# Shift-times-V summed on VectorE, the text shift made by matmul rows, the text gate moved into the output phase

## The chip, the core and the metric

The kernel runs on one core of one Trainium2 chip. The metric is the device time of one execution in microseconds (us). A profiled execution spans about 1.8 us less than that time, because the span runs from the first instruction to the last (117.0 against 118.8 us for the profiled run of before). "Before" and "after" (the changed kernel) are the two kernels compared.

## The reference

The work is an attention block with two token streams, image (256 tokens) and text (32), for B = 2 batches, with D = 1152 and all data in bf16:

```
mod_i, mod_t = silu(c) @ wmod_img, silu(c) @ wmod_txt       # shift, scale, gate of each stream
hi = layernorm(x_img) * (1 + sci) + shi ;  ht = layernorm(x_txt) * (1 + sct) + sht
qkv_i = hi @ wqkv_img ;  qkv_t = ht @ wqkv_txt
q, k, v = concat(text, image)                               # 288 tokens
a = softmax(q @ k.T * D**-0.5) @ v
out_i = x_img + gai * (ai @ wo_img) ;  out_t = x_txt + gat * (at @ wo_txt)
```

Twelve weight blocks of 1152 x 1152 are modulation or projection blocks and two are output blocks. Each is 2.65 MB, and together they are 37 of the 41 MB that a run moves.

## The kernel before

Each weight block goes into one of five slots. A load into a slot must wait until the last reader of its earlier content is done, so the table of slots is also a table of waits (in the profile they are waits of SyncE, which issues the loads: the longest in after was 12.8 us, for matmuls that read the slot):

```python
w_sc_i = wtile(0); w_v_i = wtile(1)
w_sh_i = load_w(2, wmod_img, 0)
w_q_i = load_w(3, wqkv_img, 0)
w_sh_t = load_rows(0, wmod_txt, 0)
w_k_i = load_w(4, wqkv_img, D)
w_sc_t = load_w(1, wmod_txt, D)          # waits for w_v_i
w_q_t = load_w(2, wqkv_txt, 0)           # waits for w_sh_i
w_k_t = load_w(3, wqkv_txt, D)           # waits for w_q_i
w_ga_i = load_w(0, wmod_img, 2 * D)      # waits for w_sh_t
w_v_t = load_w(1, wqkv_txt, 2 * D)
w_ga_t = load_w(2, wmod_txt, 2 * D)
w_o_i = load_rows(3, wo_img, 0)
w_o_t = load_rows(1, wo_txt, 0)
```

The image V is made without its shift, to start early. The missing term s = shi @ Wv is the same for each token of a batch, and softmax rows sum to 1, so s can be added as a bias to the attention output. The text tokens have no such term, so s is subtracted from the text V. Before gets s on TensorE, and gets the *text* shift as a sum on VectorE (DVE), folded by 16 small matmuls:

```python
def mod_rows_of(w, lhs):                          # 36 matmuls, four column groups side by side
    gps = ps_tr.tile([P, KT, LW], f32, tag="tr")
    for kt in range(KT):
        for g in range(NGG):
            mm(gps[LW*g:LW*g+LW], lhsT=lhs[:, kt, :], rhs=group(w, kt, g), ...)
    return gps
def shift_v_rows():
    p_sv = mod_rows_of(w_v_i, shT32)              # shift @ Wv on TensorE
    nc.scalar.copy(svr[:], p_sv[:])
    cols["v"] = mod_cols_of(p_sv, "svc")
def vec_part(eng, w, acc, r0, r1, bs): ...        # text shift: 18 multiply-adds on DVE over w_sh_t
def v_txt(r):
    ...                                           # 18 matmuls for the text V, then
    for g in range(2):                            # two that subtract s inside PSUM
        mm(ps[64*g:64*g+NTT], lhsT=sel[:, 2*r+g, :], rhs=svr[:], start=False, stop=True, ...)
...
vt = [v_txt(r) for r in range(2)]
v_txt_out(0, vt[0]); p_transposes(0); p_transposes(1); v_txt_out(1, vt[1])
txt_gate()                                        # 36 matmuls, then gate rows through DRAM
for d0 in range(0, KT, 3): attn_pair(...)
out_img(0, C3); out_img(1, C3); out_img(2, C3); out_txt(); out_img(3, ...)
```

## Time and profile before

| what | number | where it is read |
|---|---|---|
| time | 118.58 us, median of 5 | timing runs |
| TensorE (PE) busy | 111.2 of 117.0 us | first part of the page |
| weight queue busy | 87% of the span | DMA queues on the page |
| PE stages near the attention | below | timeline of PE |

These lines are from the page of before: the busy time of each engine, then rows of the span cut into 40 slices of 2.9 us. PE and DMA are tenths of the slice, where 9 is 90% or more; GB/s is what the DMA engines moved.

```profile
PE 111.2 (95%) x1046; PEld 63.9 (55%) x1054; DVE 74.6 (64%) x158; ACT 44.4 (38%) x91; POOL 11.1 (10%) x34
PE   4998899999999999999999999999999999999990
DMA  3999999999999999999999999999999999520223
GB/s 98 368 374 390 409 407 409 411 410 414 411 399 372 410 410 413 404 411 413 413 410 413 414 402 414 414 401 414 408 406 411 406 401 376 177 100 6 101 50 101
```

PE is full from the sixth slice on. The weight stream is full too: about 400 to 414 GB/s, with one dip to 372, until slice 33.

The next lines are from the timeline of PE in before. The columns are start in us, length in us, then engine, line, operation, tile written, tiles read and count.

```profile
64.25 1.29 PE L61 MATMUL gps<-t,sT 128*32 128x288 bf16 x36
65.36 0.66 PE L61 MATMUL gps<-hl,pick 128*32 128x288 bf16 x16
66.18 3.83 PE L61 MATMUL ps<-xT_i,t 128*128 128x512 bf16 x17 [0.16 <-issue]
...
86.64 1.29 PE L61 MATMUL gps<-t,sT 128*32 128x288 bf16 x36
87.85 0.91 PE L61 MATMUL aps<-pT,v_i 128*128 128x288 bf16 x6
88.69 0.42 PE L61 MATMUL aps<-pT,v_t 32*128 32x288 bf16 x6
89.04 1.65 PE L61 MATMUL aps<-pT,v_i 128*128 128x288 bf16 x12
```

The 36 matmuls at 86.64 are the text gate. The attention (tiles aps) follows at 87.85; its small matmuls on v_t, the text V, take 0.35 us from start to next start. Nothing waits.

These lines are from the DMA view of before: issuing queue, size of each transfer, and median us from issue to landing.

```profile
gbf<-mod_scratch POOLq DMA_DIRECT2D x4, 36.0 KB, 4.8
mod_scratch<-g_sb POOLq DMA_DIRECT2D x4, 2.2 KB, 6.1
```

### The profile page before, as it was taken

What the parts mean: (1) busy time and instruction counts of PE and PEld (TensorE: products, weight loads), DVE (VectorE), ACT (ScalarE), POOL (GpSimd) and SP (SyncE); (2) the same over time, 40 slices, a digit from 0 to 9 for tenths busy, and PEclk for the clock granted to TensorE, in tenths of its full rate; (3) what the DMA queues carried; (4) which work ended last, traced back from release to release, by engine and by line L of the source; (5) the groups of instructions that cost most, each with busy time, mean ns of one, the idle gap of its engine ahead of it and who ended that gap; (6) DMA issues with size and microseconds to landing.
All of it is one profiled execution on the core that took longest, in us unless ns stands there. A gap on an engine that the chain in (4) does not pass through costs nothing.

```text
span 117.0 us, 2513 instructions
## 1 busy us (share of the span) xinstructions
PE 111.2 (95%) x1046; PEld 63.9 (55%) x1054; DVE 74.6 (64%) x158; ACT 44.4 (38%) x91; POOL 11.1 (10%) x34
## 2 busy tenths in 40 slices
PE   4998899999999999999999999999999999999990
PEld 1245544445574444445444658777876666656660
DVE  2368694053867979999996350018984756666671
ACT  4599720042654834325265224245556610000000
POOL 7230000000000000000000000001318018000000
PEclk9999999999999999999999999999999999999998
DMA  3999999999999999999999999999999999520223
GB/s 98 368 374 390 409 407 409 411 410 414 411 399 372 410 410 413 404 411 413 413 410 413 414 402 414 414 401 414 408 406 411 406 401 376 177 100 6 101 50 101
DMA packets 18613, 40.86 MB, mean 349 GB/s; under 512 B 1019, under 2 KB 1547, under 8 KB 18603
## 3 DMA queue, kind: packets, MB, share of 16 engines
q1 hardware_dynamic: 17728, 39.56, 87.0%
q0 software_dynamic: 480, 0.89, 2.1%
q10 hardware_dynamic: 395, 0.26, 0.7%
q8 instruction: 8, 0.13, 0.4%
q14 instruction: 2, 0.02, 0.0%
HBM read 39.38 MB, written 1.34 MB: 348 GB/s over the span
## 4 chain that ended last, share of the span: by engine, by line
PE 85%; ACT 5%; DMA 4%; DVE 2%; issue 1%; DVEq 0%
PE ps L61 53%; PE vps L61 15%; PE gps L61 6%; PE aps L61 5%; PE sps L61 4%; DMA x_i<-in_x_img_dram 4%; ACT xn_i L202 2%; ACT xn_i L201 2%; PE pT_ps L64 1%; DVE xn_i L216 1%; PE tp L64 1%; DVE tmp L690 1%; ACT rstd L211 1%; ACT rstd L212 1%; DVE o L691 0%
## 5 line engine op out<-in xcount | busy, mean ns | idle before, releaser
L61 PE MATMUL ps<-xT_i,t 128*128 128x512 bf16 x157 | 35.2, 380 | 0.4 <-issue 0.2
L61 PEld LDWEIGHTS <-t 128*128 128x128 bf16 x324 | 20.5, 98 | 19.1 <-issue 0.5
L427 DVE SCALAR_TENSOR_TENSOR acc_sh<-t,sTf,acc_sh 128x1152 f32<-128x1152 bf16 x16 | 21.4, 1414 | 0.0
L61 PE MATMUL ps<-t,aT 128*128 128x384 bf16 (+3 forms) x153 | 20.2, 308 | 0.0
L61 PE MATMUL vps<-t,hS_i 128*128 128x512 bf16 (+1 forms) x106 | 17.8, 325 | 0.2
L61 PEld LDWEIGHTS <-aT 128*128 128x128 bf16 (+1 forms) x153 | 13.0, 101 | 7.1 <-issue 0.5
L61 PEld LDWEIGHTS <-hS_i 128*128 128x128 bf16 x108 | 9.0, 98 | 8.8 <-DVE hS_i L268 0.5
L690 DVE TENSOR_TENSOR tmp<-ps,gb 128x384 bf16<-128x384 f32 (+2 forms) x13 | 6.8, 526 | 6.3 <-PE ps L61 6.3
L370 ACT CAST qkT<-ps 128x512 bf16<-128x512 f32 (+2 forms) x11 | 6.0, 552 | 11.0 <-PE ps L61 11.0
L61 PE MATMUL wps<-warm 128*128 128x512 bf16 x24 | 8.1, 498 | 1.7 <-DVE unit L132 1.5
L515 POOL DMA_DIRECT2D mod_scratch<-g_sb x4 | 2.5, 633 | 74.6 <-ACT g_sb L513 74.5
L368 ACT ACTIVATE qkT<-ps 128x512 bf16<-128x512 f32 (+2 forms) x11 | 6.1, 559 | 9.1 <-PE ps L61 9.1
L184 DVE CAST v_i<-vps 128x512 bf16<-128x512 f32 x5 | 3.5, 692 | 7.5 <-PE vps L61 7.5
L554 DVE TENSOR_REDUCE nmx<-sps 128x1 f32<-128x288 f32 x4 | 1.8, 458 | 9.9 <-PE sps L61 9.9
L186 ACT CAST v_i<-vps 128x512 bf16<-128x512 f32 x4 | 2.3, 578 | 10.0 <-PE vps L61 10.0
L623 DVE TENSOR_SCALAR aT<-aps,svc 128x288 bf16<-128x288 f32 x9 | 4.3, 518 | 2.5 <-PE aps L61 2.5
L61 PEld LDWEIGHTS <-warm 128*128 128x128 bf16 x25 | 2.7, 118 | 5.5 <-issue 2.9
L61 PEld LDWEIGHTS <-sT 128*32 128x32 bf16 x180 | 4.6, 96 | 2.0 <-issue 1.3
L61 PE MATMUL sps<-qkT 128*128 128x288 bf16 (+1 forms) x54 | 5.5, 287 | 0.0
L61 PE MATMUL gps<-t,sT 128*32 128x288 bf16 x144 | 5.2, 287 | 0.0
L61 PE MATMUL aps<-pT,v_i 128*128 128x288 bf16 x36 | 5.1, 288 | 0.0
L61 PE MATMUL ps<-hT_t,t 128*128 128x64 bf16 x162 | 5.1, 193 | 0.0
(114 smaller groups left out, 109.2 us busy)
## 6 DMA issues: line engine op xcount, KB each, us to landing
t<-in_wqkv_txt_dram SPq DMA_DIRECT2D x3, 2592.0 KB, 17.8
t<-in_wmod_img_dram SPq DMA_DIRECT2D x2, 2592.0 KB, 13.0
t<-in_wqkv_img_dram SPq DMA_DIRECT2D x2, 2592.0 KB, 20.1
t<-in_wmod_txt_dram SPq DMA_DIRECT2D x2, 2592.0 KB, 15.9
t<-in_wmod_txt_dram SPq DMA_DIRECT2D x3, 864.0 KB, 14.7
t<-in_wo_img_dram SPq DMA_DIRECT2D x3, 864.0 KB, 12.8
t<-in_wo_txt_dram SPq DMA_DIRECT2D x3, 864.0 KB, 12.6
t<-in_wqkv_img_dram SPq DMA_DIRECT2D x3, 576.0 KB, 9.1
```

Source lines behind the costliest of these rows:

```text
L61: return pin(nc.tensor.matmul(*a, **k))
L64: return pin(nc.tensor.transpose(*a, **k))
L184: nc.vector.tensor_copy(out_ap, in_ap)
L186: nc.scalar.copy(out_ap, in_ap)
L201: pin(nc.scalar.activation(junk, x_ap, ACT.Copy, scale=1.0 / D, accum_out=sm[:, 0:1]))
L202: pin(nc.scalar.activation(junk, x_ap, ACT.Square, scale=float(D) ** -0.5, accum_out=sm[:, 1:2]))
L368: nc.scalar.mul(out_ap, in_ap, SCALE)
L370: nc.scalar.copy(out_ap, in_ap)
L427: pin(eng.scalar_tensor_tensor(acc[:, b, :], w[:, kt, :], sTf[:, kt, b:b + 1], acc[:, b, :], op0=ALU.mult, op1=ALU.add))
L515: nc.gpsimd.dma_start(gsc[si, b, :].rearrange("(g j) -> g j", g=NGG), g_sb[b:P:32, :])
L623: nc.vector.tensor_scalar(dst, tiles[(b, dt)][:], bias, None, op0=ALU.add)
L690: nc.vector.tensor_mul(tmp[:, 0:n], ps[:, 0:n], gb[:, b, c0:c0 + n])
```

## The change

The intent: TensorE is the bound (95% busy), and DVE has idle time (64% busy), so shift-times-V (36 matmuls) moves to DVE. The author held that DVE has no time for two such sums, so the text shift goes back to TensorE. Cut to its core:

```diff
-    w_sc_t = load_w(1, wmod_txt, D)
-    w_q_t = load_w(2, wqkv_txt, 0)
-    w_k_t = load_w(3, wqkv_txt, D)
-    w_ga_i = load_w(0, wmod_img, 2 * D)
+    w_sc_t = load_w(2, wmod_txt, D)
+    w_q_t = load_w(3, wqkv_txt, 0)
+    w_k_t = load_w(0, wqkv_txt, D)
+    w_ga_i = load_w(2, wmod_img, 2 * D)
     w_v_t = load_w(1, wqkv_txt, 2 * D)
-    w_ga_t = load_w(2, wmod_txt, 2 * D)
-    w_o_i = load_rows(3, wo_img, 0)
-    w_o_t = load_rows(1, wo_txt, 0)
+    w_o_i = load_rows(4, wo_img, 0)
+    w_ga_t = load_w(3, wmod_txt, 2 * D)
+    w_o_t = load_rows(0, wo_txt, 0)
 ... (w_q_i now in three pieces, w_sh_t in one)
-    def shift_v_rows(): ...                       # and the DVE sum of the text shift
+    def sv_part(r0, r1): ...                      # 18 DVE multiply-adds over w_v_i into acc_sv
+    def sv_blocks(): ...                          # per batch a 32x32 block transpose and a reduce_sum
+    def sv_fold(): ...                            # two matmuls with `fold`; gives svc, the bias
+    def sv_rows():
+        ps = ps_tr.tile([B * KT, P], bf, tag="tr", name="svr")
+        tr(ps[:], svcb[:].rearrange("p b k -> p (b k)"), ident[:])
+        pin(nc.scalar.copy(srow[:], ps[:]))
+        nc.gpsimd.dma_start(svd[:, :].rearrange("b (k p) -> (b k) p", p=P), srow[:])
+        for g in range(2):
+            for b in range(B):
+                r0 = 64 * g + NT * b
+                nc.gpsimd.dma_start(svb[r0:r0 + NT, :], svd[b, g * HD:(g + 1) * HD].partition_broadcast(NT))
     def txt_rows_shift():
-        ...                                       # 16 fold matmuls
+        rows["sh"] = mod_rows_of(w_sh_t, sT32)
     def v_txt_out(r, ps):
-        ...                                       # copies; the two sel matmuls of v_txt go too
+        pin(nc.vector.tensor_sub(v_t[:, r * VC:(r + 1) * VC], ps[:], svb[:, r * VC:(r + 1) * VC]))
+        if r == 0:
+            pin(nc.vector.tensor_sub(v_t[0:NTT, HD:HD + NTT], ps[NTT:P, 0:NTT], svb[NTT:P, 0:NTT]))
 ...
-    qk_img(w_q_i, 0, {1: (txt_stats, txt_shift_part(0, 3),), 3: (txt_norm,), 4: (txt_shift_part(3, 6),),
-                      7: (txt_shift_part(6, KT),)})
-    qk_img(w_k_i, 1, {1: (txt_transposes, txt_shift_split,),
-                      6: (txt_rows_scale, txt_rows_shift, txt_cols_shift, txt_modulate),
-                      8: (lambda: qk_txt(0, w_q_t),)})
+    qk_img(w_q_i, 0, {0: (txt_stats, sv_part(0, 3)), 3: (txt_norm,), 4: (sv_part(3, 6),), 8: (sv_part(6, KT),)})
+    qk_img(w_k_i, 1, {1: (txt_transposes,),
+                      3: (txt_rows_scale, txt_rows_shift, txt_cols_shift, txt_modulate, sv_blocks),
+                      8: (lambda: qk_txt(0, w_q_t), sv_fold)})
+    sv_rows()
     qk_txt(1, w_k_t)
 ...
-    v_txt_out(0, vt[0]); p_transposes(0); p_transposes(1); v_txt_out(1, vt[1]); ...
-    txt_gate()
+    p_transposes(0)
+    for r in range(2):
+        v_txt_out(r, v_txt(r))
+    p_transposes(1)
     attention
     out_img(0, C3)
+    txt_gate()
     out_img(1, C3)
```

The sum s now reaches the text V through DRAM (store, then four broadcast loads into svb). And w_v_i stays in its slot until DVE is done with it, so the later blocks had to change slots.

More of the change, by code (lines that the diff above doesn't have):

```diff
@@ L111 @@
     w_sh_i = load_w(2, wmod_img, 0)
-    w_q_i = load_w(3, wqkv_img, 0)
-    w_sh_t = load_rows(0, wmod_txt, 0)
+    w_q_i = load_rows(3, wqkv_img, 0)
+    w_sh_t = load_w(0, wmod_txt, 0)
     w_k_i = load_w(4, wqkv_img, D)
-    w_sc_t = load_w(1, wmod_txt, D)
-    w_q_t = load_w(2, wqkv_txt, 0)
-    w_k_t = load_w(3, wqkv_txt, D)
-    w_ga_i = load_w(0, wmod_img, 2 * D)
+    w_sc_t = load_w(2, wmod_txt, D)
+    w_q_t = load_w(3, wqkv_txt, 0)
+    w_k_t = load_w(0, wqkv_txt, D)
+    w_ga_i = load_w(2, wmod_img, 2 * D)
     w_v_t = load_w(1, wqkv_txt, 2 * D)
-    w_ga_t = load_w(2, wmod_txt, 2 * D)
-    w_o_i = load_rows(3, wo_img, 0)
-    w_o_t = load_rows(1, wo_txt, 0)
+    w_o_i = load_rows(4, wo_img, 0)
+    w_ga_t = load_w(3, wmod_txt, 2 * D)
+    w_o_t = load_rows(0, wo_txt, 0)
     nc.scalar.preload_act_table_set("natural_log_exp_and_others")
@@ L144 @@
     sTf = const.tile([P, KT, B], f32)
-    pick = const.tile([P, B, 32], bf)
-    nc.gpsimd.memset(pick[:], 0.0)
-    for b in range(B):
-        nc.gpsimd.memset(pick[:, b, b:b + 1], 1.0)
-    shT32 = const.tile([P, KT, 32], bf)
-    nc.gpsimd.memset(shT32[:], 0.0)
     PBW = 3 * P
@@ L162 @@
     nc.gpsimd.tensor_copy(ident2[:, P - NT:P], ident[:, 0:NT])
+    fold = const.tile([P, NGG, LW], bf)
+    nc.gpsimd.tensor_add(fold[:, 0, :], ident[:, 0:LW], ident[:, LW:2 * LW])
+    for g in range(2, NGG):
+        nc.gpsimd.tensor_add(fold[:, 0, :], fold[:, 0, :], ident[:, g * LW:(g + 1) * LW])
+    for g in range(1, NGG):
+        nc.gpsimd.tensor_copy(fold[:, g, :], fold[:, 0, :])
     e18 = small.tile([B * KT, P], f32, bufs=1)
@@ L227, in mod_cols_of @@
     def mod_cols_of(gps, name):
-        t = const.tile([P, KT, LW], f32, name=name, tag={"shtc": "scc", "sctc": "shc"}.get(name, name))
+        t = const.tile([P, KT, LW], f32, name=name, tag={"shtc": "scc"}.get(name, name))
         pin(nc.vector.transpose(t[:].rearrange("p c l -> p (c l)"), gps[:].rearrange("p c l -> p (c l)")))
@@ L344 @@
     sh_i = mod_cols_of(p_sh, "shc")
-    nc.vector.tensor_copy(shT32[:, :, 0:B], sh_i[:, :, 0:B])
     hT_i = xT_i
@@ L382 @@
     gsc = tc.dram_tile([2, B, D], bf, name="mod_scratch")
-    sel = const.tile([P, NGG, NTT], bf)
-    nc.gpsimd.tensor_scalar(sel[:].rearrange("p g (b t) -> p g b t", b=B),
-                            ident[:].rearrange("p (g r) -> p g r", g=NGG)[:, :, 0:B].unsqueeze(3)
-                            .to_broadcast([P, NGG, B, NT]), -1.0, None, op0=ALU.mult)
-    v_t = act.tile([P, D], bf)
-    svr = act.tile([P, KT, LW], bf)
+    svd = tc.dram_tile([B, D], bf, name="sv_scratch")
+    HD = D // 2
+    v_t = act.tile([P, HD + NTT], bf)
+    svb = act.tile([P, HD], bf)
     rows, cols = {}, {}
-    def shift_v_rows():
-        p_sv = mod_rows_of(w_v_i, shT32)
-        nc.scalar.copy(svr[:], p_sv[:])
-        cols["v"] = mod_cols_of(p_sv, "svc")
     xT_t = act.tile([P, KT, NTT], bf)
@@ L402, in txt_stats @@
     def txt_stats():
-        junk = v_t[0:NTT, :]
+        junk = work.tile([P, D], bf, tag="o", name="junk")[0:NTT, :]
         pin(nc.scalar.activation(junk, x_t[:], ACT.Copy, scale=1.0 / D, accum_out=sm_t[0:NTT, 0:1]))
@@ L419, in txt_transposes @@
             nc.scalar.copy(xT_t[:, k0:k1, :], tpt[:, 0:k1 - k0, h, :])
-    def vec_part(eng, w, acc, r0, r1, bs):
-        for kt in range(r0, r1):
-            for b in bs:
-                if kt == 0:
-                    pin(eng.tensor_scalar(acc[:, b, :], w[:, kt, :], sTf[:, kt, b:b + 1], None, op0=ALU.mult))
-                else:
-                    pin(eng.scalar_tensor_tensor(acc[:, b, :], w[:, kt, :], sTf[:, kt, b:b + 1], acc[:, b, :],
-                                                 op0=ALU.mult, op1=ALU.add))
@@ L430, in vec_split @@
-    def vec_split(acc):
-        hl = work.tile([P, 2, B, D], bf, tag="hl", bufs=1, name="hl")
-        halves[acc.name] = hl
-        for b in range(B):
-            nc.scalar.copy(hl[:, 0, b, :], acc[:, b, :])
-            pin(nc.vector.tensor_sub(hl[:, 1, b, :], acc[:, b, :], hl[:, 0, b, :]))
-        return hl
-    def vec_rows(hl, gps, strip):
-        terms = [(b, t) for b in range(B) for t in range(2)]
-        for b, t in terms:
-            for g in range(NGG):
-                mm(gps[LW * g:LW * g + LW], lhsT=pick[:, b, :], rhs=strip(hl[:, t, b, :], g),
-                   start=((b, t) == terms[0]), stop=((b, t) == terms[-1]), tile_position=(0, LW * g))
-        return gps
@@ L446, with sv_part, run @@
-    halves = {}
-    acc_sh = act.tile([P, B, D], f32, tag="Bt")
-    def txt_shift_part(r0, r1):
-        return lambda: vec_part(nc.vector, w_sh_t, acc_sh, r0, r1, range(B))
-    def txt_shift_split():
-        vec_split(acc_sh)
+    acc_sv = act.tile([P, B, D], f32, tag="Bt")
+    def sv_part(r0, r1):
+        def run():
+            for kt in range(r0, r1):
+                for b in range(B):
+                    acc, col = acc_sv[:, b, :], sh_i[:, kt, b:b + 1]
+                    if kt == 0:
+                        pin(nc.vector.tensor_scalar(acc, w_v_i[:, kt, :], col, None, op0=ALU.mult))
+                    else:
+                        pin(nc.vector.scalar_tensor_tensor(acc, w_v_i[:, kt, :], col, acc,
+                                                           op0=ALU.mult, op1=ALU.add))
+        return run
@@ new lines, with sv_blocks @@
+    NB = D // LW
+    uf = small.tile([P, B, NB], f32, tag="uf", bufs=1)
+    ub = small.tile([P, 2, B, NB], bf, tag="ub", bufs=1)
+    svc = const.tile([P, B, KT], f32)
+    svcb = const.tile([P, B, KT], bf)
+    srow = const.tile([B * KT, P], bf)
+    def sv_blocks():
+        for b in range(B):
+            blk = work.tile([P, NB, LW], f32, tag="blk", bufs=1, name="blk")
+            pin(nc.vector.transpose(blk[:].rearrange("p c l -> p (c l)"), acc_sv[:, b, :]))
+            pin(nc.vector.reduce_sum(uf[:, b, :], blk[:], axis=AX.X))
+        pin(nc.vector.tensor_copy(ub[:, 0], uf[:]))
+        pin(nc.vector.tensor_sub(ub[:, 1], uf[:], ub[:, 0]))
@@ new lines, in sv_fold @@
+    def sv_fold():
+        ps = ps_tr.tile([P, B, KT, NGG], f32, tag="tr", name="svps")
+        for h in range(2):
+            mm(ps[:].rearrange("p b k a -> p (b k a)"), lhsT=fold[:].rearrange("p g l -> p (g l)"),
+               rhs=ub[:, h].rearrange("p b c -> p (b c)"), start=(h == 0), stop=(h == 1))
+        for a in range(NGG):
+            pin(nc.vector.tensor_copy(svc[LW * a:LW * a + LW], ps[LW * a:LW * a + LW, :, :, a]))
+        pin(nc.vector.tensor_copy(svcb[:], svc[:]))
+    def sv_rows():
[4 more added lines that the diff above has]
+        for g in range(2):
+            for b in range(B):
+                r0 = 64 * g + NT * b
+                nc.gpsimd.dma_start(svb[r0:r0 + NT, :], svd[b, g * HD:(g + 1) * HD].partition_broadcast(NT))
@@ L455, in txt_rows_shift @@
     def txt_rows_shift():
-        gps = ps_tr.tile([P, KT, LW], f32, tag="tr")
-        rows["sh"] = vec_rows(halves[acc_sh.name], gps,
-                              lambda a, g: a.rearrange("p (c g l) -> p g c l", g=NGG, l=LW)[:, g])
+        rows["sh"] = mod_rows_of(w_sh_t, sT32)
     def txt_cols_shift():
@@ L489, in v_txt, with v_txt_cols @@
     def v_txt(r):
-        ps = ps_mm.tile([P, KT, LW], f32, tag="mm")
+        ps = ps_mm.tile([P, VC], f32, tag="mm")
         for kt in range(KT):
             for g in range(2):
-                mm(ps[64 * g:64 * g + NTT], lhsT=hT_t[:, kt, :], rhs=group(w_v_t, kt, 2 * r + g),
-                   start=(kt == 0), stop=False, tile_position=(0, 64 * g))
-        for g in range(2):
-            mm(ps[64 * g:64 * g + NTT], lhsT=sel[:, 2 * r + g, :], rhs=svr[:],
-               start=False, stop=True, tile_position=(0, 64 * g))
+                c0 = g * HD + r * VC
+                mm(ps[64 * g:64 * g + NTT, :], lhsT=hT_t[:, kt, :], rhs=w_v_t[:, kt, c0:c0 + VC],
+                   start=(kt == 0), stop=(kt == KT - 1), tile_position=(0, 64 * g))
         return ps
     def v_txt_out(r, ps):
-        for g in range(2):
-            dst = v_t[0:NTT, :].rearrange("p (c g l) -> p g c l", g=NGG, l=LW)[:, 2 * r + g]
-            src = ps[64 * g:64 * g + NTT]
-            pin(nc.vector.tensor_copy(dst, src))
+        pin(nc.vector.tensor_sub(v_t[:, r * VC:(r + 1) * VC], ps[:], svb[:, r * VC:(r + 1) * VC]))
+        if r == 0:
+            pin(nc.vector.tensor_sub(v_t[0:NTT, HD:HD + NTT], ps[NTT:P, 0:NTT], svb[NTT:P, 0:NTT]))
+    def v_txt_cols(b, dt):
+        h, c0 = (1, dt * P - HD) if dt > KT // 2 else (0, dt * P)
+        r0 = 64 * h + NT * b
+        return r0, v_t[r0:r0 + NT, c0:c0 + P]
     def mod_rows(w_blk, si):
@@ L536 @@
     v_last()
-    shift_v_rows()
-    qk_img(w_q_i, 0, {1: (txt_stats, txt_shift_part(0, 3),), 3: (txt_norm,), 4: (txt_shift_part(3, 6),),
-                      7: (txt_shift_part(6, KT),)})
-    qk_img(w_k_i, 1, {1: (txt_transposes, txt_shift_split,),
-                      6: (txt_rows_scale, txt_rows_shift, txt_cols_shift, txt_modulate),
-                      8: (lambda: qk_txt(0, w_q_t),)})
+    qk_img(w_q_i, 0, {0: (txt_stats, sv_part(0, 3)), 3: (txt_norm,), 4: (sv_part(3, 6),), 8: (sv_part(6, KT),)})
[3 more added lines that the diff above has]
+    sv_rows()
     qk_txt(1, w_k_t)
@@ L594, in p_transposes @@
     def p_transposes(b):
-        pT_ps = ps_tr.tile([P, 8 * P], bf, tag="tr")
-        def one(kj, pb, qp, perm):
-            o = kj * NTOK + qp
-            tr(pT_ps[:, o:o + P], pb[:, kj * P:(kj + 1) * P], perm[:])
-        for kj in range(3):
-            if b:
-                one(kj, pbs["t"], qpos[b][2], ident2)
-            for qi in range(TPB):
-                one(kj, pbs[(b, qi)], qpos[b][qi], ident)
-            if not b:
-                one(kj, pbs["t"], qpos[b][2], ident)
-        pT_v = pT_ps[:, 0:3 * NTOK].rearrange("p (k n) -> p k n", k=3)
-        pT = work.tile([P, 3, NTOK], bf, tag="pT")
-        pin(nc.scalar.copy(pT[:], pT_v))
+        pT = work.tile([P, 3, NTOK], bf, tag="pT")
+        tiles = [(range(3), ps_tr)] if b == 0 else [((2,), ps_mm), (range(2), ps_tr)]
+        for kjs, pool in tiles:
+            pT_ps = pool.tile([P, 8 * P], bf, tag="tr" if pool is ps_tr else "mm", name="pT_ps")
+            txt = [(2, pbs["t"], ident2 if b else ident)]
+            img = [(qi, pbs[(b, qi)], ident) for qi in range(TPB)]
+            for n, kj in enumerate(kjs):
+                for qi, pb, perm in (txt + img if b else img + txt):
+                    o = n * NTOK + qpos[b][qi]
+                    tr(pT_ps[:, o:o + P], pb[:, kj * P:(kj + 1) * P], perm[:])
+            pin(nc.scalar.copy(pT[:, kjs[0]:kjs[-1] + 1, :],
+                               pT_ps[:, 0:len(kjs) * NTOK].rearrange("p (k n) -> p k n", n=NTOK)))
         pTs[b] = pT
@@ L620, in attn_evac @@
         for b, dt in tiles:
-            dst, bias = aT[:, dt, b * NTOK:(b + 1) * NTOK], cols["v"][:, dt, b:b + 1]
+            dst, bias = aT[:, dt, b * NTOK:(b + 1) * NTOK], svc[:, b, dt:dt + 1]
             if evac_idx[0] % 2 == 0:
@@ L633, in attn_pair @@
             first, (b, dt) = key in t1, key
-            r0 = 64 * (n // 2 % 2) + NT * b
-            mm((t1 if first else t0)[key][:], lhsT=v_t[r0:r0 + NT, dt * P:(dt + 1) * P],
+            r0, vcols = v_txt_cols(b, dt)
+            mm((t1 if first else t0)[key][:], lhsT=vcols,
                rhs=pTs[b][r0:r0 + NT, 2, :], start=first, stop=not first, tile_position=(r0, 0))
@@ L668 @@
     img_div(I[3])
-    vt = [v_txt(r) for r in range(2)]
-    v_txt_out(0, vt[0])
     p_transposes(0)
+    for r in range(2):
+        v_txt_out(r, v_txt(r))
     p_transposes(1)
-    v_txt_out(1, vt[1])
-    pin(nc.vector.tensor_copy(v_t[64:64 + NTT, :], v_t[0:NTT, :]))
-    txt_gate()
-    for d0 in range(0, KT, 3):
-        attn_pair(*[[(b, dt) for dt in range(d0, d0 + 3)] for b in range(B)])
+    for dts in ((0, 5, 1), (6, 2, 7), (3, 8, 4)):
+        attn_pair(*[[(b, dt) for dt in dts] for b in range(B)])
     def out_img(i, chunks, parts=None):
```

## The prediction

> **What bounds the kernel now.** TensorE. The page of the profile gives PE busy 111.2 of 117.0 us (95%), and the chain that ended last is 85% PE; in the timeline PE has no gap over 0.2 us from 14.5 us to the end. The weight stream runs almost level with it: queue q1 is busy 87% of the span and the DMA row stays at 99% until 96 us. The DMA issues show w_ga_t landing at 85.7 us (read at 86.6) and the last third of w_o_i at 93.0 (read at 93.6).
>
> **PE work removed (timeline).** Shift-times-V rows, 33.51 to 34.73: 1.22 us. The 16 matmuls that fold the text shift, 65.36 to 66.18 with the gap: 0.82. The two pairs of sel matmuls in the text V: about 0.24. Together 2.3 us.
>
> **Added.** Text-shift rows as 36 matmuls, 1.15 us like the text-scale rows at 64.25. Fold (2 small matmuls) and one transpose: about 0.15. Net PE saving about 1.0 us, of which 0.7 before the attention. The text gate (1.2 us) moves but stays.
>
> **VectorE.** 18 multiply-adds of 1.37 us stay, on w_v_i instead of w_sh_t (estimate: done at 59 us). The two hl subtractions and the two casts on ACT go; two 1152-wide block transposes and two reductions come (estimate 5 us, from the 128x288 transpose of 0.48). All in DVE idle time, before 70 us. Off the path.
>
> **Weight stream.** w_v_i's slot is now held until 59 us, so the next loads go to other slots. w_q_t can start only when w_q_i was read (51 us), w_k_t only after the text-shift rows (59.4). I expect one hole of about 2 us in the DMA near 60. w_v_t should then land near 81, still ahead of its read (83); w_o_i now goes ahead of w_ga_t. No PE stall from this.
>
> **The new wait.** -shift@V now reaches the text V through DRAM: transpose at 73.5, store at 74.6, then four broadcast loads into svb. Before, the 2 KB stores to the scratch took 5.4 us at 81 us, and the 36 KB gate loads 3.8 to 5.2. [...] So estimate: stored by 80, loaded by 86 to 87, v_t complete 1.3 us later, as two subtractions must also free the PSUM buffers of the second half of the attention tiles. PE, relieved of the text gate there, would want v_t at about 86.5. Stall: 0.7 to 1.5 us. Also, p_transposes(0) now come right after the scores, about 0.4 us before pbt is ready (83.35 before); part of the same wait.
>
> **Tail.** gb lands about 1 us later (behind svb in the POOL queue), and its first reader comes earlier: a DVE wait at the start of the output, absorbed by six PSUM buffers. gbf lands near 108, about when the text output needs it.
>
> **Sum.** -1.0 + 0.4 + 0.8 = about +0.2 us: 118.8 us, range 117.6 to 120.1. Same 0.91, faster by 2% 0.03, slower by 2% 0.06.
>
> **Right if** PE busy falls by about 1 us, and the PE waits show v_t or svb-caused idle of about 1 us just before the first v_t matmuls near 87 us, with svb landing at 86 to 87. **Wrong if** svb lands before 85 (then 118.1), or after 88 (then 120); if the DMA hole pushes w_v_t past 83 or w_ga_t past 97 (slower); or if the DVE sum ends much after 62, delaying hT_t and w_v_t's slot.

Store and loads were estimated from the times measured in before (5.4 us, and 3.8 to 5.2), and the sum stays -1.0 + 0.4 + 0.8 = +0.2 us.

## More of the kernel before

A 2 KB store to DRAM took 6.1 us (median of four, issued at 81.5 to 89.2 us, while the core moved 410 GB/s from 81 to 93 us). A 36 KB load took 4.8 us (median of four, issued at 96.1 to 98.3 us, as the weight stream ended: 386 GB/s from 96 to 99 us, 168 from 99 to 103).

## The result, and the profile after

After took 120.6 us, median of 5 runs (119.86 to 121.91), and before took 118.58 beside it. The ratio of fast runs is 1.0134, with a 95% interval of 1.0100 to 1.0169. A ratio here is always the mean time of one kernel's fast runs over that of the other's in the same rounds, so it is not quite the ratio of the medians. Two of the five runs of after are labelled slow: they had a mean granted TensorE clock of 0.986, and took 121.8 to 121.9. The other three took 119.86, 120.08 and 120.6. The whole interval lies above 1: about 1.6 us were lost (1.34% of 118.58) where 0.2 had been predicted. The median of all five runs lies above the predicted range, which ended at 120.1; the three fast runs alone, with a mean of 120.18 us and a median of 120.08, lie at its upper edge. So the range was missed narrowly, and the size of the loss clearly.

The same rows from the page of after:

```profile
PE 111.2 (94%) x1029; PEld 63.9 (54%) x1037; DVE 77.0 (65%) x163; ACT 42.4 (36%) x90; POOL 13.5 (11%) x40
PE   4999799999999999999999999999959999999990
DMA  3999999999999999999969999999999999934223
GB/s 107 364 366 388 408 404 412 409 411 410 410 390 342 413 410 410 412 304 368 412 168 390 399 389 390 405 404 412 401 387 413 415 417 400 402 131 98 99 50 99
```

Two things are new. PE has a slice of 5 near 88 us. The GB/s row has dents: 304 and 368 (slices 18 and 19, near 52 us) and 168 (slice 21, near 60 us). The stream lasts longer: slice 35 is now at 402.

The timeline of PE in after, at the same stages:

```profile
57.45 2.39 PE L61 MATMUL gps<-t,sT 128*32 128x288 bf16 x72
60.00 9.66 PE L61 MATMUL ps<-xT_i,t 128*128 128x512 bf16 x44 [0.16 <-issue]
...
86.33 0.90 PE L61 MATMUL aps<-pT,v_i 128*128 128x288 bf16 x6
88.50 0.55 PE L61 MATMUL aps<-pT,v_t 32*128 32x288 bf16 x3 [1.27 <-DVE v_t L503]
89.24 0.30 PE L61 MATMUL aps<-pT,v_t 32*128 32x288 bf16 x3 [0.19 <-DVE v_t L503]
89.47 1.65 PE L61 MATMUL aps<-pT,v_i 128*128 128x288 bf16 x12
```

The attention starts at 86.33, 1.5 us earlier than before. Then it waits for v_t at 88.50, and once more at 89.24. From its first matmul to the twelve of the second group it takes 3.14 us (89.47 - 86.33), against 1.19 before (89.04 - 87.85): a stall of 1.95 us.

The chain of work that ended last in after (start, length, what) shows where v_t was:

```profile
75.10 5.57 DMA sv_scratch<-srow
80.67 0.29 issue
80.97 1.50 POOL svb L459 x3
82.47 5.39 DMA svb<-sv_scratch
87.88 0.05 DVEq L503
87.98 0.46 DVE v_t L503
88.47 0.23 DVE v_t L505
88.73 0.47 DVE v_t L503
```

The store took 5.57 us, the last of the four loads was issued at 82.47 and took 5.39, and three DVE subtractions took 1.2. In before the same term was already in PSUM.

Where the 1.4 us went can be summed from the timelines. The clock of each trace is set to its first matmul of the image-shift rows (28.23 us before, 28.58 after). The traces of the kernels reach that point between 27.94 and 28.86 us, without order, so it is scatter of the start and not the change.

| stage, from the first shift row on | before | after | difference |
|---|---|---|---|
| to the first attention matmul | 59.62 | 57.74 | -1.88 (of it -1.21: the gate moved away) |
| attention | 5.79 | 7.74 | +1.95 |
| output, to the start of its last matmul | 19.95 | 21.28 | +1.33 (of it +1.22: the gate) |
| sum | 85.36 | 86.76 | +1.40 |

The gate apart, TensorE gained 0.67 us up to the attention, and lost 1.95 us waiting there.

### The profile page after: what moved, and what is told of

Same layout as the page of the kernel before. It is cut to its first block, busy times and chain, and to the rows that moved or that the text cites. A ratio compares the mean times of both kernels' runs of the same rounds, so it can differ in the third digit from the quotient of the medians.

```text
span 118.7 us, 2495 instructions
## 1 busy us (share of the span) xinstructions
PE 111.2 (94%) x1029; PEld 63.9 (54%) x1037; DVE 77.0 (65%) x163; ACT 42.4 (36%) x90; POOL 13.5 (11%) x40
## 3 DMA queue, kind: packets, MB, share of 16 engines
q0 software_dynamic: 640, 1.05, 2.8%
HBM read 39.52 MB, written 1.34 MB: 344 GB/s over the span
## 4 chain that ended last, share of the span: by engine, by line
PE 73%; DMA 18%; DVE 2%; issue 1%; POOL 1%; SPq 1%; ACT 1%; DVEq 0%
PE ps L61 48%; PE vps L61 15%; DMA t<-in_wmod_img_dram 9%; DMA sv_scratch<-srow 5%; DMA svb<-sv_scratch 5%; PE aps L61 4%; PE gps L61 4%; POOL svb L459 1%; PE sc_ps L61 1%; DVE v_t L503 1%; SPq L104 1%; PE tp L64 1%; DVE tmp L688 1%; ACT qkT L369 0%; DVE o L689 0%
## 5 line engine op out<-in xcount | busy, mean ns | idle before, releaser
L423 DVE SCALAR_TENSOR_TENSOR acc_sv<-t,shc,acc_sv 128x1152 f32<-128x1152 bf16 x16 | 21.4, 1415 | 0.0
L455 POOL DMA_DIRECT2D sv_scratch<-srow x1 | 0.7, 694 | 68.2 <-ACT srow L454 68.2
L61 PEld LDWEIGHTS <-sT 128*32 128x32 bf16 x216 | 5.6, 96 | 3.0 <-issue 2.2
L61 PE MATMUL gps<-t,sT 128*32 128x288 bf16 x180 | 6.3, 287 | 0.0
L626 ACT ACTIVATE aT<-aps,svc 128x288 bf16<-128x288 f32 x9 | 4.1, 499 | 3.4 <-PE aps L61 3.3
```

The lines of the kernel that those rows point to most:

```text
L61: return pin(nc.tensor.matmul(*a, **k))
L423: pin(nc.vector.scalar_tensor_tensor(acc, w_v_i[:, kt, :], col, acc, op0=ALU.mult, op1=ALU.add))
L626: nc.scalar.activation(dst, tiles[(b, dt)][:], ACT.Identity, bias=bias)
```

## The experiments

Two theories stood. **W**: the way of s through DRAM holds up the attention. **D**: the weight stream is late, because the new slots leave holes in it; in after this is hidden behind W, since PE arrives late anyway. Rivals: **G**, moving the gate is itself the cost; **S**, the start is later (0.35 us in the profile).

### The first batch

a_again is after, unchanged.

> The changed kernel once more, unchanged, to have its time and a second trace beside the variants. Theory W (the way of shift-times-V through DRAM holds up the attention): 120.1 us in fast runs, first v_t matmul again about 1.4 us late and the second group of tiles another 0.6 us late, with svb landing at 87 to 88. The rival S (a later start: the first scale weights landed 0.5 us later in the first trace) expects the start of the text V again 0.3 us later than it would be by the removed work; if the early weights land as in the kernel before this time and the total stays over 119.8, S falls.

It took 121.71 us (120.86 to 122.64), beside 118.8 for before. The ratio of 1.0235 is inflated: three of its six runs had a clock of 0.986. The other three have a mean of 121.23 us, 1.020 times before's mean of 118.82. svb landed at 86.4 to 87.6, and the stall was there again. Rows of the image shift began at 28.32, so S falls as a cause of the loss.

a_early makes the fold earlier and sends the store off about 2 us sooner:

```diff
-                      8: (lambda: qk_txt(0, w_q_t), sv_fold)})
-    sv_rows()
+                      8: (sv_fold, lambda: qk_txt(0, w_q_t), sv_rows)})
```

> The fold of the sum is put before the text queries and its rows right after them, so that the store leaves about 2.1 us earlier; the work is the same. W alone: svb lands near 85.7, the 2.0 us stall goes, time 118.2. W with the weight stream as the next limit (theory W+D: holes in the DMA near 52 and 60 us made w_ga_t land at 98.0, just when the gate wanted it): the gate then waits 1.0 to 1.5 us for w_ga_t, time 119.2 to 119.5. The rival G (moving the gate is itself what costs) expects no gain: 120.1.

It took 121.0 us, ratio 1.0185 (1.0136 to 1.0233). svb landed at 83.7 to 85.0 and the wait for v_t was gone, yet nearly nothing was gained. W alone fails here. The number of W+D (119.2 to 119.5, with a wait for w_ga_t alone) was missed too, and G's 120.1 came nearest; b_gate, below, rules G out. The profiled execution (122.16 us) was one of the slower ones.

a_free takes the wait away with wrong data: pinned order, and the input c as the source of the loads.

```diff
-                nc.gpsimd.dma_start(svb[r0:r0 + NT, :], svd[b, g * HD:(g + 1) * HD].partition_broadcast(NT))
+                pin(nc.gpsimd.dma_start(svb[r0:r0 + NT, :], c[b, g * HD:(g + 1) * HD].partition_broadcast(NT)))
```

> Wrong result on purpose: the four svb loads read the input c in place of the stored sum and are issued right behind the store, without waiting for its landing. Same instructions, same bytes. svb then lands about 5 us earlier, near 83. W: no v_t wait at all, 118.1. W+D: the gate waits about 1.4 us for w_ga_t instead, 119.4. G: 120.1.

It took 120.5 us, ratio 1.0152 (1.0113 to 1.019), with a wrong result. svb landed at 80.8 to 82.3. These lines are the waits of PE in a_free (who waited, for what, us in total, times, longest):

```profile
PE ps L61 <- DMA t<-in_wqkv_txt_dram: 1.1, 1, 1.1
PE gps L61 <- DMA t<-in_wmod_txt_dram: 1.1, 1, 1.1
```

There is no wait for v_t. In its place PE waits for w_v_t (read by the text V at 84.0) and later for w_ga_t. The stall moved to the weight stream: D. In a_early the wait for w_v_t was 2.0 us and that for w_ga_t 1.1. The time missed the 119.4 of W+D here too, because the wait for w_v_t had not been foreseen. W did not hide that wait: the text V comes before the wait for v_t, and after read w_v_t at 83.49 without waiting. The stream itself was later in these two executions: counted from the first shift row, w_k_t landed 1.8 us later in a_free than in after, and 2.6 us later in a_early, before the store of s was issued.

b_gate is before with only the gate moved:

```diff
-    w_ga_t = load_w(2, wmod_txt, 2 * D)
     w_o_i = load_rows(3, wo_img, 0)
+    w_ga_t = load_w(2, wmod_txt, 2 * D)
 ...
-    txt_gate()            # ahead of the attention
 ...
     out_img(0, C3)
+    txt_gate()
```

> The kernel before with the text gate alone moved behind the first output tile, and w_o_i loaded ahead of w_ga_t as that needs. G: over 119.6. W and W+D: the gate covered about 0.4 us of the copy of pT on ScalarE, which now shows before the attention: 118.6 to 119.1, and no wait for w_ga_t, which lands near 92.5.

It took 119.26 us, ratio 1.0033 (1.0005 to 1.0062), between the two expected ranges. The waits of PE show what the gate had covered:

```profile
PE aps L61 <- ACT pT L610: 0.5, 1, 0.5
```

G falls as the cause: the move costs 0.4 us here, through the exposed copy of pT. After splits that copy in two and shows no such wait.

### The second batch: fill the stream, cut the way

a_nohole keeps the stream full. The text-shift rows are made earlier, so that w_sh_t gives its slot back at about 46 us; the blocks after it trade slots:

```diff
-    w_q_t = load_w(3, wqkv_txt, 0)
-    w_k_t = load_w(0, wqkv_txt, D)
+    w_q_t = load_w(0, wqkv_txt, 0)
+    w_k_t = load_w(3, wqkv_txt, D)
 ... (w_ga_t into slot 0, w_o_t into slot 3)
-    qk_img(w_q_i, 0, {..., 4: (sv_part(3, 6),), 8: (sv_part(6, KT),)})
+    qk_img(w_q_i, 0, {..., 4: (sv_part(3, 6),), 6: (txt_rows_shift, txt_cols_shift), 8: (sv_part(6, KT),)})
-                      3: (txt_rows_scale, txt_rows_shift, txt_cols_shift, txt_modulate, sv_blocks),
+                      3: (txt_rows_scale, txt_modulate, sv_blocks),
```

> The changed kernel with its weight stream kept full: the text-shift rows are made during the image queries (hook 6), so that w_sh_t's slot is free near 46 us; w_q_t goes there and w_k_t into w_q_i's slot. svb still goes through DRAM at the same place. Theory D+W (two limits side by side: holes of 1.5 to 1.9 us in the stream, and the DRAM way of svb): the DMA idle time between 46 and 100 us falls under 0.4 us, but the v_t wait of 2.0 us stays and the time is that of the changed kernel within 0.5 us, near 2.0% over the kernel before. D alone (the stream is the whole cause): time within 0.5% of the kernel before.

It took 120.65 us, ratio 1.0157 (1.0132 to 1.0182). The GB/s row of its page has no such dents:

```profile
GB/s 118 371 371 374 394 405 410 407 410 414 411 402 385 412 409 412 412 406 411 411 413 412 411 404 413 414 404 409 402 388 411 418 414 232 80 143 31 99 50 99
```

But its waits of PE still hold the one for v_t:

```profile
PE aps L61 <- DVE v_t L503: 1.2, 2, 1.0
```

Curing D alone gains little here, as curing W alone did in a_early and a_free.

a_selnohole is a_nohole with the DRAM way replaced. Matmuls with a small selection matrix add -s into the PSUM of the text V:

```diff
+    sel = const.tile([B * KT, KT, NTT], bf)          # -1 where row (b, k) belongs to batch b of the token
 ... (svd, svb and their DMAs go)
+        for n in range(3):
+            for g in range(2):
+                c0 = g * HD + r * VC
+                k = c0 // P + n
+                lo, hi = max(c0, k * P), min(c0 + VC, (k + 1) * P)
+                mm(ps[64 * g:64 * g + NTT, lo - c0:hi - c0], lhsT=sel[:, k, :], rhs=srow[:, lo - k * P:hi - k * P], ...)
-        pin(nc.vector.tensor_sub(v_t[:, r * VC:(r + 1) * VC], ps[:], svb[:, r * VC:(r + 1) * VC]))
+        pin(nc.vector.tensor_copy(v_t[:, r * VC:(r + 1) * VC], ps[:]))
```

> As a_nohole, and the way through DRAM is replaced by 12 small matmuls that add the sum's rows to the text V in PSUM with a selection matrix. Both limits gone. D+W: no wait for v_t, w_v_t or w_ga_t over 0.3 us; the removed PE work shows: 118.2 to 118.7, at or up to 0.4% under the kernel before. If a third limit is hidden, the time stays over 119.5.

It took 118.94 us, ratio 1.0033 (1.0007 to 1.0059): the loss is nearly gone, a little outside the expected range. The 12 extra matmuls eat what was saved: its attention starts 0.66 us later after the first shift row than that of the next variant (58.63 against 57.97).

a_earlynohole joins a_nohole and a_early, with s still going through DRAM.

> As a_nohole, with the fold and its rows made earlier as in a_early; svb still through DRAM, landing near 85. D+W: no v_t wait over 0.3 us, w_v_t and w_ga_t in time: 118.2 to 118.8. In a_early alone the same reordering gave little, as the stream was late; if D is right the same edit is worth 1.5 to 2 us here.

It took 118.87 us, just over the expected range, ratio 1.0007 (0.9979 to 1.0035). svb landed at 82.8 to 84.1, and PE shows no wait for v_t or for a weight near the attention or the gate. The page of a_earlynohole:

```profile
PE   4999799999999999999999999999999999999990
GB/s 122 359 374 376 400 405 409 408 410 411 411 405 381 411 413 409 415 403 411 413 409 413 413 405 412 413 405 408 381 402 412 423 406 397 163 124 59 101 51 101
```

The edit of a_early, worth nearly nothing with holes in the stream (1.0185 against 1.020), takes the ratio from 1.0157 to 1.0007 without them. That is the mark of two waits side by side: this cure shows only when the other is in place. (With the selection matmuls about half of the loss goes even with the holes there; see a_sel and the square.)

b_slots tests D on the old arithmetic. It is b_gate with the slots and load order of after (the diff of the load table above, but with w_q_i and w_sh_t loaded in the pieces of before), and nothing else.

> b_gate (the kernel before with the gate moved, 119.3) with the changed kernel's slots and load order, and nothing else of the change: w_q_t waits for the image queries, w_k_t for the VectorE shift sum that frees w_sh_t. D: holes near 53 and 62 us as in the changed kernel, 1.5 to 2.5 us; w_v_t lands near 85, 2 us after it is wanted, and w_ga_t near 98 to 99: 121 to 122. W alone: no slowdown, 119.3.

It took 121.02 us, ratio 1.0187 (1.016 to 1.0215), against 1.0033 for b_gate. The GB/s row of its page:

```profile
GB/s 110 376 401 388 396 404 409 412 414 410 412 375 398 413 409 414 402 174 318 415 162 335 401 392 401 408 400 414 397 410 424 404 408 410 405 132 103 99 50 99
```

And one of its waits of PE:

```profile
PE ps L61 <- DMA t<-in_wqkv_txt_dram: 1.7, 1, 1.7
```

The slots alone make the holes and the wait for w_v_t. In this kernel w_sh_t is freed by DVE, and its holes are a little larger than in after (314 GB/s against 341 between 46 and 62 us). (The result came out at the low end of "121 to 122"; w_ga_t was hardly late.)

### The third batch: is there a version that beats both?

a_best is a_earlynohole with half of the text V ahead of the first transposes, and a_earlynohole2 repeats a_earlynohole:

```diff
-    p_transposes(0)
-    for r in range(2):
-        v_txt_out(r, v_txt(r))
+    v_txt_out(0, v_txt(0))
+    p_transposes(0)
+    v_txt_out(1, v_txt(1))
```

> a_earlynohole (118.9, level with the kernel before) with the first half of the text V put ahead of the first transposes, which wait about 0.15 us for the text probabilities. Theory D+W with nothing hidden: at most 0.2 us better than a_earlynohole, 118.5 to 118.9, so not clear of the kernel before; the saved PE work is only about 0.35 us.

> a_earlynohole once more beside a_best, to narrow its interval: 118.5 to 119.0, ratio to the kernel before between 0.997 and 1.003.

a_best took 118.65 us, ratio 1.0003 (0.9974 to 1.0031), and a_earlynohole2 took 118.54, ratio 0.9992 (0.9964 to 1.0021). Neither is clear of before. On the clock of the table above, a_earlynohole takes 85.01 us to before's 85.36, in both of its traces: with all stalls cured, the change is worth 0.35 us of TensorE time, 0.3% of the run, which the timing does not resolve.

a_sel is after with the selection matmuls and its own slots.

> The changed kernel with the selection matmuls in place of the DRAM way, but its own slots and load order: the last corner of the square. D+W: no v_t wait, but w_v_t 1 to 2 us late and w_ga_t about 1 us late: 120.2 to 121. W alone: 118.5.

It took 119.54 us, ratio 1.009 (1.0046 to 1.0135), better than expected: w_v_t came in time, and only w_ga_t was late (0.4 us). So curing W alone is worth something where w_v_t is in time.

### The square, on one chip

The corners had been run on different chips, so all four were run again beside each other.

> Corner 1 of the square, all four on one chip beside each other: the changed kernel, DRAM way and holes both there. D+W: 120.1 to 121.3, 1.3 to 2.3% over the kernel before.

> Corner 2: DRAM way gone, holes there. D+W, two limits that overlap: part of the loss goes, 119.3 to 120.2, the rest being waits for w_v_t or w_ga_t. If the two costs simply add up, this corner and corner 3 must lie above corner 4 by shares that sum to corner 1's excess.

> Corner 3: DRAM way there, holes gone. D+W: the v_t wait of about 2 us stays, 120.2 to 120.9, little better than corner 1.

> Corner 4: both gone. D+W: 118.5 to 119.1, within 0.5% of the kernel before.

| ratio to before (95% interval), fast runs | holes in the stream | stream full |
|---|---|---|
| s through DRAM | 1.0144 (1.0108 to 1.0181) | 1.0128 (1.0105 to 1.0152) |
| s by selection matmuls | 1.0079 (1.0042 to 1.0117) | 1.0039 (1.0018 to 1.0061) |

Against the lower right corner, the DRAM way alone costs 0.89%, the holes alone 0.40%, both 1.05%. The costs overlap: both come to less than the sum of 1.29%, though the intervals are too wide to settle how much. W is the larger in this square, but the size of D differs from pair to pair: b_slots lies 1.5% over b_gate, and a_early 1.8% over a_earlynohole, while W costs 1.5% between a_nohole and a_earlynohole. Which of the two is larger in general stays open. In this batch the stream-limited corner waited for w_ga_t 0.5 us, as these lines of the waits of q_sel show:

```profile
PEld L61 <- DMA t<-in_wmod_txt_dram: 0.9, 1, 0.9
PE gps L61 <- DMA t<-in_wmod_txt_dram: 0.5, 1, 0.5
```

q_after (120.9 us), q_nohole (120.48) and q_sel (119.9) met their expectations; q_selnohole (119.27, expected up to 119.1) was slightly over it.

### The slow executions of after

In 8 of the 29 executions of kernels that keep the long wait for v_t (after, a_again, q_after, a_nohole, q_nohole) the mean clock was 0.986, and they took 121.8 to 122.6 us. None of the 66 executions of the other variants, and none of the 44 executions of before beside them, shows it. Three such executions were profiled. This one is q_after; the windows view gives, for each stretch, its length, then busy us (and count) of PE, PEld, DVE, ACT and POOL, then PEclk, DMA share and GB/s.

```profile
86.60:89.00 2.40, 0.82 (x8) 0.32 (x8) 1.46 (x4) 0.50 (x1) 0.68 (x2) 1.00 1.05 410
90.20:93.50 3.30, 3.30 (x19) 1.58 (x17) 1.62 (x4) 1.39 (x3) 0.00 (x0) 0.50 1.04 417
```

And its timeline of PE:

```profile
88.97 2.00 PE L61 MATMUL aps<-pT,v_i 128*128 128x288 bf16 x12
...
91.49 2.62 PE L61 MATMUL aps<-pT,v_i 128*128 128x288 bf16 x12
```

After a stretch of 2.4 us with 0.82 us of PE work, the granted clock is 0.50 for a while: by the clock record from 90.11 to 93.52, 3.41 us. Twelve attention matmuls then take 2.62 us where after at full clock takes 1.65. The other two traces show the same: from 89 to 93 and from 93 to 96 us the mean clock (windows view) is 0.59 and 0.98 in a_again, and 0.73 and 0.79 in q_nohole, which comes to 3.4 us at half clock in each. In q_after a wait of 1.4 us at the longest for v_t, in a_again of 1.3 and in q_nohole of 1.6 preceded it.

The clock records offer a reason why only some executions are hit; it was not tested. In the records of before, after and q_after the clock changes lie on a grid with steps of 3.41 us: in before the record begins at 6.61 us, and the one change, at 115.84, is 32 steps later; in after it begins at 7.16, and the one change, at 119.80 (behind the last instruction), is 33 steps later; in q_after it begins at 4.78 us, and 90.11, 93.52 and 120.83 are 25, 26 and 34 steps later. Where the grid begins differs from trace to trace, so it falls differently on the same wait. These are the windows view of the step just before the half clock in q_after, and of the emptiest step near the wait in after:

```profile
86.70:90.11 3.41, 1.93 (x16) 1.21 (x17) 2.25 (x6) 1.44 (x3) 1.14 (x2) 1.00 1.04 410
85.67:89.08 3.41, 2.11 (x22) 1.20 (x19) 1.04 (x3) 1.23 (x3) 0.17 (x1) 1.00 1.05 384
```

The step holds 1.93 us of PE work in q_after, which was hit, and 2.11 in after, which kept the full clock. The length of the wait does not sort them: a_again, which was hit, and after have the same waits of 1.27 and 0.19 us. But PE's busy time does not sort them alone: b_slots kept the full clock after a stretch of 3.41 us with 1.68 us of it (81.71 to 85.12, with the wait of 1.7 us for w_v_t in it). What brings the half clock stays open, and no run moved the grid on purpose. a_early waits for 2.0 us too, in another place, and none of its six runs was hit. In these runs, then, the lower mean clock came only in kernels that keep the long wait for v_t (8 of 29 executions, against none of 110 others), and not in each of their executions.

## Why the prediction was wrong

The mechanism named as the new wait was right. Its size, the saving set against it, and one "no stall" were not.

- **"Stall: 0.7 to 1.5 us", taken as 0.8 in the sum.** This is the main step that failed. The stall was 1.95 us. The parts were good: store 5.57 us (taken as 5.4), v_t complete 1.3 us after svb. But the prediction's own times (svb at 86 to 87, v_t complete 1.3 us later, wanted at 86.5) come to 0.8 to 1.8 us, and the sum took the low end. And the parts follow each other, each a little late: the store left at 75.10 and not 74.6 (0.35 of this is the later start of the trace, which PE shares), the last load landed at 87.9 and not at 86 to 87.
- **"Net PE saving about 1.0 us".** Up to the attention it was 0.67 us, and 0.35 us over the whole kernel with the stalls cured. The fold was booked at 0.82 us "with the gap". In b_slots, where none of these records is missing, its 16 matmuls take 0.59 us from their start to the next matmul's. In before's trace the group behind it shows x17 of 18: the "gap" was one lost record. The new fold and transpose cost about 0.3 us, not 0.15. PE busy on the page did not fall at all (111.2 both times).
- **"No PE stall from this" (the weight stream).** In the trace of after this holds to the letter: w_v_t came in time, but w_ga_t only because PE was already late. w_ga_t landed at 98.03 us, past the 97 that the prediction itself names as "slower", and the gate read it at 98.55. So without the stall for v_t PE could have won at most 0.52 us there before it waited for w_ga_t; q_sel, on the clock of the table above, takes 86.24 us, 0.52 less than after. There were two dents and not one hole, though the prediction names both late loads (w_q_t at 51, w_k_t at 59.4). Between 46 and 62 us (windows view) the core moved 341 GB/s against 411 before; over 16 us that is 1.1 MB, or 2.7 us at the old rate. With the wait for v_t removed, PE waited for w_ga_t instead (a_sel, q_sel), and in a_free and a_early for w_v_t too. The stream had been level with PE in before (408 GB/s with PE busy 81.0 of 81.5 us), so it had no slack to give.
- **"if svb lands before 85 (then 118.1)".** a_early and a_free are that case, and took 121.0 and 120.5.
- **The half-clock executions** were not foreseen. They set two of the five runs of the result.
- **Right:** the place of the stall; the DVE sum (done at 59.1, estimated 59); the two-step release of the attention tiles; the gate as neutral in its own work; the tail as harmless, though gbf landed at 109.7 and not near 108, and gb did not land later than before. The wait of 0.4 us that was predicted for pbt did not show: the waits of PE list none over 0.2 us there.

Some things stay open. The block after the second hole, w_k_t, landed between 68.4 and 72.0 us in the traces of after and its variants with these slots, though it was issued within 1 us (59.2 to 60.1). This scatter goes with how late w_v_t comes: where w_k_t landed by 70.1 us, PE waited 0.2 us or less for w_v_t; where it landed at 70.3 and 72.0 (a_free, a_early), and at 71.8 in b_slots, PE waited 1.1, 2.0 and 1.7. Its cause was not found: the edit of a_free first acts at the store of s, after w_k_t has landed, so it is not that. The landing of w_v_t itself is missing from the traces.

After the holes the stream also ran a little below its rate although the DMA engines were as busy as before (1.04 in the windows view of both before and after): 392 GB/s (after), 387 (a_early) and 399 (b_slots) between 64 and 74 us, against 410 in before and in a_earlynohole. Why is not known.

## What to carry to other kernels

When two resources run level, as TensorE and the weight stream did here, removing work from one while lengthening the life of a buffer that the other needs may be no gain (here it cost 1.34%), and a wait that you can see may hide the next one behind it: test the cures together before you judge either. Be wary of sending a value that is wanted soon through DRAM beside a full DMA queue: in after the 4.5 KB store took 5.57 us and the 36 KB loads 5.4 to 5.8 us beside the weight stream, while 36 KB loads with the stream over (gbf) took 2.4 us. Count store plus load at their measured loaded times (11 to 13 us here from the first issue to the last landing), and start the chain early. Write down each buffer's last reader before and after a change: the load table is a dependency graph.
